# A compact recurrent state summed in TensorE, routing pieces put behind the expert units, the first gathers spread, early weight splits on GpSimd

## The chip, the cores and the metric

The kernel runs on one core of a Trainium2 chip. The metric is the device time of one execution in microseconds (us). The core has five engines that run side by side, each in the order of its own program: TensorE (PE in the rows, its weight loads PEld), VectorE (DVE), ScalarE (ACT), GpSimd (POOL) and SyncE (SP), which issues most transfers. An engine that reaches an instruction whose operands are not ready stands still, and all that is queued behind it on that engine stands too.

## The reference

Three parts follow one another (the numbers: 4 batches, 8 heads, 768 positions, head dimension 48, so 3072 tokens of 384 values):

```
state = f * state + k (x) v ;  y = q . state          # gated recurrence, per head, f = sigmoid(f_logit)
logits = x @ w_gate + softplus(x @ w_noise) * noise   # 8 experts, the two best of each token, softmax of the two
out[token] += weight * (relu(x @ w1[e]) @ w2[e])      # 384 -> 1024 -> 384 for each chosen expert
xn = x / rms(x) * g ;  (silu(xn @ wg) * (xn @ wv)) @ wo    # 384 -> 1536 -> 384 for every token
```

## The kernel before

**The recurrence** is done in 24 chunks of 128 positions, six to a batch (`gla_stream`, chunk number i). Two stages run ahead of the chunk: `decay` (VectorE `ft`, ScalarE twice, a scan on VectorE into `cs`) four chunks ahead, and `prep` (ScalarE exponentials, VectorE products `KT` and `QT`) two chunks ahead. In the chunk itself TensorE makes `scores`, transposes the next keys (`keys`), turns the last result into rows (`rows`), applies the carried state (`inter`), sums the chunk's own state (`state`) and applies the masked scores (`attend`); VectorE masks the scores (`AM`), and the state is carried on in `carry`: VectorE adds the new sum in PSUM and the old state for each half of the partitions (`su`, two instructions), GpSimd multiplies by the decay `hs` (two more). The state tile `Ss` is 128 partitions by 4 by 2 by 64 with zeros where the two heads of a pair don't meet, so that `inter` is four products over all 128 rows.

**The experts** work in units: a block is up to 512 tokens of one expert, a unit is 128 hidden columns of it. A unit has a first product `l1` (nine matmuls at 256 tokens, since a 32-bit product is done as three products of split halves, `hi` and `lo`), then ScalarE makes `hhi` and VectorE `hlo`, and two units later the second product `l2` (L646 in both). A first product needs a free PSUM bank, which the `hlo` of an earlier unit releases. Weights come in as `raw`, ScalarE makes `whi` and `wlo` is the difference (L211). Tokens of an expert are gathered from the recurrence's result `xd` by indirect transfers that GpSimd issues (L721), four to 128 tokens, then VectorE transposes them (`xt`, L732) and they are split into `xhi` and `xlo`.

**The routing** (`router`, a generator that stops at pieces) finds the two experts of each token, their places, and the lists for the gathers. It runs twice: for the first 8 chunks during the recurrence (`ahead`, one piece at each `safe()`, of which there are three to a chunk; the list ROUTE says at which chunk), and for the other 16 after it (`rest`, one piece to a unit by the list `jobs`). Both go through `route`, which raises their priority by 50. The pieces with `r_ol` and `r_rh` build one-hot tables on VectorE.

**What sets the order.** TensorE's order is the program's own (`manual_schedule`); the other engines' order is made by a list scheduler from dependences and priorities; `issue_after` keeps an instruction from being placed before another, `paced` makes a transfer wait for `mark[0]`, the last unit's `hhi`. Until the first block's tokens are there, the recurrence runs alone (`banks[0]` is BANK); then units are put between its steps in proportion to the costs that `gla_stream` yields (SHARED), and after chunk 23 the units run alone (FULL). The first block's gathers are issued from chunk FETCH on (12), its transposes at chunk 14.

## Time and profile before

| | |
|---|---|
| median of 3 runs | 1113.02 us (1111.37 to 1114.33) |
| the profiled execution | 1108.8 us, its span 1107.0 us |
| TensorE busy | 1045.5 us, 94% of the span |
| VectorE busy | 685.8 us, 62% |
| ScalarE, GpSimd busy | 483.3 us, 354.0 us |
| chain of waits that ended last | TensorE 74%, VectorE 6%, DMA 4%, issue 2% |

The shares are means over stages with different limits. In the page's 40 slices (27.7 us each) TensorE is below nine tenths in the first four, in the eighth and ninth (194 to 249 us) and in the last; elsewhere it is busy. So the stages have to be read one by one. Three of them matter here: the recurrence alone (to about 111 us), recurrence and units together (to about 207 us), and the first units alone (to about 260 us).

### The profile page before, as it was taken

To read this page: it belongs to the slowest core of one execution; us is meant where nothing else is said; L and a number is where in the kernel's file an instruction comes from. 1 tells how busy PE (TensorE), PEld (TensorE's weight loads), DVE (VectorE), ACT (ScalarE), POOL (GpSimd) and SP (SyncE) were. 2 spreads that over 40 slices of the span, in tenths; PEclk is the share of its full clock that TensorE was granted. 3 is DMA by queue.
4 is the path that set the end of the run, shared out by engine and by line. 5 is a ranking of instruction groups with operands and counts; after the bars stand their busy time and mean duration, and the time that the engine had idled before them with its cause. 6 is when DMAs were issued, how large, how long until landed. Compare 5 with 4: busy or idle time off the path is not lost.

```text
span 1107.0 us, 18624 instructions
## 1 busy us (share of the span) xinstructions
PE 1045.5 (94%) x6897; PEld 953.0 (86%) x6897; DVE 685.8 (62%) x1529; ACT 483.3 (44%) x1092; POOL 354.0 (32%) x384
## 2 busy tenths in 40 slices
PE   7885999869999999999999999999999999999997
PEld 5765899869999999999999988788888888888886
DVE  7997876688777555555676769645345444354332
ACT  6764654435665443444454544523223223232211
POOL 3344654344353434555546433220030020110000
PEclk8998899989999999999999999999999999999999
DMA  9987463357685543444353534020020110110000
GB/s 282 302 271 211 146 194 120 118 172 236 217 268 191 159 128 104 137 164 129 125 159 117 159 126 130 30 72 15 1 86 1 44 44 1 57 29 1 29 1 32
DMA packets 105256, 132.96 MB, mean 120 GB/s; under 512 B 9088, under 2 KB 81172, under 8 KB 105156
## 3 DMA queue, kind: packets, MB, share of 16 engines
q1 hardware_dynamic: 95587, 112.25, 31.5%
q0 software_dynamic: 9568, 19.43, 6.5%
q8 instruction: 56, 0.92, 0.3%
q14 instruction: 45, 0.36, 0.1%
HBM read 107.63 MB, written 24.02 MB: 119 GB/s over the span
## 4 chain that ended last, share of the span: by engine, by line
PE 74%; DVE 6%; DMA 4%; issue 2%; ACT 1%; POOL 0%; SPq 0%; DVEq 0%; ACTq 0%; POOLq 0%
PE bank L646 70%; DMA raw<-in_moe_w_dram 2%; DVE wlo L211 1%; PE bank L173 1%; DMA xg<-xd,stokr 1%; PE bank L443 1%; PE scores L379 1%; PE bank L431 1%; PE bank L421 1%; DMA xg<-xd,stoka 1%; DVE hlo L750 1%; DVE xt L732 0%; POOL xg L721 0%; DVE xlo L634 0%; DVE cv L180 0%
## 5 line engine op out<-in xcount | busy, mean ns | idle before, releaser
L646 PE MATMUL bank<-xhi,whi 128*128 128x256 f32 (+8 forms) x1008 | 339.9, 337 | 23.2 <-DVE hlo L750 13.1
L646 PE MATMUL bank<-xlo,whi 128*128 128x256 f32 (+8 forms) x1008 | 336.3, 334 | 1.3 <-DVE xlo L634 1.3
L646 PE MATMUL bank<-xhi,wlo 128*128 128x256 f32 (+8 forms) x1008 | 336.1, 333 | 0.0
L646 PE MATMUL bank<-whi,hhi 128*128 128x384 f32 (+2 forms) x728 | 247.9, 341 | 3.6 <-ACT y L766 2.3
L646 PE MATMUL bank<-whi,hlo 128*128 128x384 f32 (+2 forms) x728 | 245.6, 337 | 0.0
L646 PE MATMUL bank<-wlo,hhi 128*128 128x384 f32 (+2 forms) x728 | 245.0, 337 | 0.0
L646 PEld LDWEIGHTS bank<-xhi,whi 128*128 128x128 f32 x1008 | 191.5, 190 | 46.8 <-DVE hlo L750 15.2
L646 PEld LDWEIGHTS bank<-xlo,whi 128*128 128x128 f32 x1008 | 191.6, 190 | 17.9 <-DVE xlo L634 2.3
L646 PEld LDWEIGHTS bank<-xhi,wlo 128*128 128x128 f32 x1008 | 191.6, 190 | 17.4
L721 POOL DMA_INDIRECT xg<-xd,stokr x139 | 136.4, 981 | 151.6 <-ACT hhi L749 119.2
L750 DVE SCALAR_TENSOR_TENSOR hlo<-bank,hhi 128x256 fp32r<-128x256 f32 (+7 forms) x192 | 83.4, 434 | 112.5 <-ACT hhi L749 88.7
L211 DVE TENSOR_TENSOR wlo<-raw,whi 128x256 fp32r<-128x256 f32 (+1 forms) x296 | 135.0, 492 | 11.8 <-ACT whi L209 6.7
L209 ACT ACTIVATE whi<-raw 128x256 fp32r<-128x256 f32 (+1 forms) x320 | 128.3, 451 | 31.9 <-DMA raw<-in_moe_w_dram 23.4
L646 PEld LDWEIGHTS bank<-whi,hhi 128*128 128x128 f32 (+2 forms) x728 | 133.4, 183 | 9.7 <-ACT y L766 2.9
L646 PEld LDWEIGHTS bank<-wlo,hhi 128*128 128x128 f32 (+2 forms) x728 | 133.3, 183 | 6.2
L646 PEld LDWEIGHTS bank<-whi,hlo 128*128 128x128 f32 (+2 forms) x728 | 132.8, 182 | 3.4
L749 ACT ACTIVATE hhi<-bank 128x256 fp32r<-128x256 f32 (+7 forms) x192 | 74.7, 389 | 138.4 <-PE bank L646 116.1
L840 DVE TENSOR_TENSOR sg<-bank,sg 128x512 f32<-128x512 f32 x72 | 49.7, 690 | 118.0 <-ACT sg L839 117.9
L791 POOL DMA_INDIRECT xg<-yd,slots x40 | 44.4, 1110 | 242.7 <-ACT hhi L843 207.6
L839 ACT ACTIVATE sg<-bank 128x512 f32<-128x512 f32 x72 | 43.2, 600 | 145.4 <-PE bank L646 136.7
L843 ACT ACTIVATE hhi<-sg 128x512 fp32r<-128x512 f32 x72 | 45.4, 631 | 116.1 <-DVE sg L841 115.9
L721 POOL DMA_INDIRECT xg<-xd,stoka x64 | 70.1, 1096 | 70.0 <-ACT hhi L749 54.5
(159 smaller groups left out, 1089.4 us busy)
## 6 DMA issues: line engine op xcount, KB each, us to landing
raw<-in_moe_w_dram SPq DMA_DIRECT2D x64, 768.0 KB
kq<-in_kq_dram SPq DMA_DIRECT2D x23, 512.0 KB
yd<-y SPq DMA_DIRECT2D x48, 192.0 KB
ft<-in_f_logit_dram SPq DMA_DIRECT2D x23, 256.0 KB
Vs<-in_v_dram SPq DMA_DIRECT2D x24, 192.0 KB
xd<-x SPq DMA_DIRECT2D x24, 192.0 KB
raw<-in_moe_w_gate_dram SPq DMA_DIRECT2D x6, 768.0 KB
raw<-in_moe_w_val_dram SPq DMA_DIRECT2D x6, 768.0 KB
```

The costliest lines, as they stand in the source:

```text
L173: nc.tensor.transpose(p, x, i)
L209: nc.scalar.activation(hi[:, j], raw[:, j], AF.Copy)
L211: e.tensor_tensor(lo[:, j], raw[:, j], hi[:, j].bitcast(F32), op=OP.subtract)
L379: nc.tensor.matmul(p[:, h % 2, h // 2, :], KT[o:o + D, h // 2, :], QT[o:o + D, h // 2, :], start=True, stop=True)
L646: nc.tensor.matmul(o, a, b, start=start and i == 0, stop=stop and i == 2)
L721: paced(nc.gpsimd.indirect_dma_start(out=b.xg[i][:, k_], out_offset=None, in_=table, in_offset=bass.IndirectOffsetOnAxis(ap=rows_of[:, k_, ...
L749: mark[0] = nc.scalar.activation(hhi[:, :N], p[:, :N], AF.Relu).ins
L750: mark[1] = nc.vector.scalar_tensor_tensor(hlo[:, :N], p[:, :N], 0.0, hhi[:, :N].bitcast(F32), op0=OP.max, op1=OP.subtract).ins
L791: paced(nc.gpsimd.indirect_dma_start(out=y, out_offset=None, in_=ya if n < GROUP else yd, in_offset=bass.IndirectOffsetOnAxis(ap=at_, axis ...
L839: nc.scalar.activation(sg, ps[0], AF.Sigmoid)
L840: nc.vector.tensor_tensor(sg, ps[0], sg, op=OP.mult)
L843: mark[0] = nc.scalar.activation(hhi, sg, AF.Copy).ins
```

## The change

It has four parts.

1. **State.** `Ss` becomes 128 by 4 by 64 with one head of a pair in each half of the partitions. `state` begins with one matmul of the old state by the identity (chunks 1 to 4 of a batch), the chunk's own products are summed onto it in PSUM, and `carry` is one VectorE instruction over 128 partitions that multiplies by the last column of `cs`. `inter` becomes eight products of 48 rows and 64 columns instead of four of 128 and 128.
2. **Early work to GpSimd.** While the recurrence runs alone, all weight splits `wlo` stand on GpSimd (before, only the first third or half of each part), and so does `QT` of every odd chunk from 3 on.
3. **First gathers and routing pieces.** The last routing piece of the first run stands at chunk 11 instead of 12; the eight gathers stand in pairs, six in chunk 12 and two in chunk 13, each waiting for a `tick` (the last `AM`, `yT` or `x`); the first transpose stands at the end of chunk 13, the second at the start of 14. The yields of a chunk are 1.1, 1.1, 1.2 instead of 0.7, 0.5, 0.5, 0.5, 1.2 (3.4 both).
4. **Late routing pieces.** The second run's pieces keep their units but lose the raised priority and are placed behind the unit's `hhi` and `hlo`.

```diff
-    ROUTE, FETCH = (8, 8, 9, 9, 10, 10, 10, 11, 12), 12
+    ROUTE, FETCH = (8, 8, 9, 9, 10, 10, 10, 11, 11), 12
...
-                    e = nc.vector if j or banks[0] is FULL else nc.gpsimd
+                    e = nc.vector if banks[0] is FULL or (j and banks[0] is SHARED) else nc.gpsimd
...
-        nc.vector.tensor_tensor(st["QT", n][:, s], cs, st["kq", n][:, s, 1], op=OP.mult)
+        e = nc.gpsimd if n % 2 and banks[0] is BANK and n > 1 else nc.vector
+        e.tensor_tensor(st["QT", n][:, s], cs, st["kq", n][:, s, 1], op=OP.mult)
...
-        pU = cut(bank("U"), HP, D)
+        st["pU", n] = pU = cut(bank("U"), HP, D)
+        if c:
+            nc.tensor.matmul(pU, ident, Ss[c % 2][:, :, :D], start=True, stop=False,
+                             skip_group_check=True)
         for a in range(HP):
             for g in range(2):
                 h = 2 * a + g
                 nc.tensor.matmul(pU[64 * g:64 * (g + 1), a], Ks[n % NK][:, h],
-                                 Vs[n % NV][:, h * D:(h + 1) * D], start=True, stop=True,
-                                 skip_group_check=True)
+                                 Vs[n % NV][:, h * D:(h + 1) * D], start=not c,
+                                 stop=True, skip_group_check=True)
...
-        for g in range(2):
-            o = slice(64 * g, 64 * (g + 1))
-            wb = hs[o, n, :, None].to_broadcast([64, HP, D])
-            sn = Ss[(c + 1) % 2][o, :, g, :D]
-            if c:
-                nc.vector.tensor_tensor(t[o], u[o], Ss[c % 2][o, :, g, :D], op=OP.add)
-                st["C"] = nc.gpsimd.tensor_tensor(sn, t[o], wb, op=OP.mult).ins
-            else:
-                nc.vector.tensor_tensor(sn, u[o], wb, op=OP.mult)
+        st["C"] = nc.vector.tensor_tensor(Ss[(c + 1) % 2][:, :, :D], st["pU", n],
+                                          st["cs", n][:, :, P - 1:].to_broadcast([P, HP, D]),
+                                          op=OP.mult).ins
...
-                nc.tensor.matmul(pY[:, a, :], Ss[c % 2][:, a].rearrange("p b d -> p (b d)"),
-                                 st["QT", n][:, a, :], start=a == 0, stop=False,
-                                 skip_group_check=True)
+                for g in range(2):
+                    o = 64 * g
+                    nc.tensor.matmul(pY[o:o + 64, a, :], Ss[c % 2][o:o + D, a],
+                                     st["QT", n][o:o + D, a, :], start=a == 0, stop=False,
+                                     skip_group_check=True)
...
-        if mark[0] is not None:
+        m = mark[0] or st.get("tick")
+        if m is not None:
...
-    for i, fn in enumerate(blocks[0].fetches + [blocks[0].turns]):
-        at(FETCH + i, lambda fns=fn: [fn() for fn in fns])
+    for i, fns in enumerate(blocks[0].fetches):
+        for o in (0, 2):
+            at(FETCH + (2 * i + o // 2) // 3, lambda fns=fns[o:o + 2]: [fn() for fn in fns])
+    at(FETCH + 1, idle)
+    at(FETCH + 1, blocks[0].turns[0])
+    at(FETCH + 2, blocks[0].turns[1])
...
+    def step():
+        with behind():
+            next(rest, None)
+
     for gap in (0, 0, 0, 0, 0, 1, 0, 0, 0, 0, 2, 1, 2, 2):
-        jobs += [lambda: route(rest)] + [idle] * gap
-    jobs += [lambda: route(rest), settle]
+        jobs += [step] + [idle] * gap
+    jobs += [step, settle]
```

How this moves the instructions is seen at three places. First VectorE in the recurrence alone, about two chunks at the place where the first weights are split, before (`su` is the sum of the state, `wlo` a weight split, `lg` the routing logits):

```order
L411 TENSOR_TENSOR su<-bank_587,Ss_131 64x192 x2
L358 TENSOR_TENSOR QT<-cs,kq 128x512
L331 TENSOR_SCALAR ft<-ft 128x512
L211 TENSOR_TENSOR wlo_751<-raw,whi_750 128x256 x2
L211 TENSOR_TENSOR wlo_833<-raw,whi_832 128x256
L383 TENSOR_TENSOR AM<-scores,mask 128x1024
L337 SCALAR_TENSOR_TENSOR cs<-chain,L 128x512
L447 TENSOR_REDUCE lg<-bank_643 128x16
L352 SCALAR_TENSOR_TENSOR KT<-Ek,kq 128x512
L358 TENSOR_TENSOR QT<-cs,kq 128x512
L331 TENSOR_SCALAR ft<-ft 128x512
L211 TENSOR_TENSOR wlo_833<-raw,whi_832 128x256
```

and of the change:

```order
L409 TENSOR_TENSOR Ss_132<-bank_593,cs 128x4x48
L337 SCALAR_TENSOR_TENSOR cs<-chain,L 128x512
L384 TENSOR_TENSOR AM<-scores,mask 128x1024
L352 SCALAR_TENSOR_TENSOR KT<-Ek,kq 128x512
L446 TENSOR_REDUCE lg<-bank_646 128x16
L331 TENSOR_SCALAR ft<-ft 128x512
L359 TENSOR_TENSOR QT<-cs,kq 128x512
```

The two `su` become one product into `Ss`, the four `wlo` have gone, and of two chunks' `QT` one is left.

Second, GpSimd from the last early splits to the first block's gathers (`hs` is a copy of the decay, the DMA rows are the gathers), before:

```order
L412 TENSOR_TENSOR Ss_132<-su,hs 64x4x48
L211 TENSOR_TENSOR wlo_1324<-raw,whi_1323 128x384
L211 TENSOR_TENSOR wlo_1409<-raw,whi_1408 128x384
L412 TENSOR_TENSOR Ss_131<-su,hs 64x4x48 x2
L360 COPY hs<-cs 128x4
L412 TENSOR_TENSOR Ss_132<-su,hs 64x4x48 x2
L360 COPY hs<-cs 128x4 x2
L721 DMA xg<-xd,stoka 128x96 x8
L360 COPY hs<-cs 128x4
```

and of the change:

```order
L211 TENSOR_TENSOR wlo_1340<-raw,whi_1339 128x384
L361 COPY hs<-cs 128x4
L211 TENSOR_TENSOR wlo_1340<-raw,whi_1339 128x384
L361 COPY hs<-cs 128x4
L211 TENSOR_TENSOR wlo_1429<-raw,whi_1428 128x384 x2
L359 TENSOR_TENSOR QT<-cs,kq 128x512
L361 COPY hs<-cs 128x4 x2
L359 TENSOR_TENSOR QT<-cs,kq 128x512
L721 DMA xg<-xd,stoka 128x96 x6
L361 COPY hs<-cs 128x4
L721 DMA xg<-xd,stoka 128x96 x2
```

The products into `Ss` have gone, whole splits and `QT` have come, and the eight gathers in a row are now six and two.

Third, VectorE in the units alone, where the one-hot tables are made (`hlo` belongs to a unit; the `hlo` before this stretch stands six rows up, with table rows alone between), before:

```order
L542 TENSOR_TENSOR r_ol<-irowh,r_hf 128x1024
L546 TENSOR_TENSOR r_rh<-r_rh,names 128x448
L544 TENSOR_TENSOR r_rh<-irowh,r_hf 128x448
L542 TENSOR_TENSOR r_ol<-irowh,r_hf 128x1024
L546 TENSOR_TENSOR r_rh<-r_rh,names 128x448
L544 TENSOR_TENSOR r_rh<-irowh,r_hf 128x448
L732 STREAM_TRANSPOSE xt<-xg 128x384
L546 TENSOR_TENSOR r_rh<-r_rh,names 128x448
L211 TENSOR_TENSOR wlo_3052<-raw,whi_3051 128x256
L634 TENSOR_TENSOR xlo_3043<-xt,xhi_3042 128x3x128
L211 TENSOR_TENSOR wlo_3052<-raw,whi_3051 128x256 x2
L750 SCALAR_TENSOR_TENSOR hlo<-bank_3061,hhi 128x256
```

and of the change, beginning with a unit's `hlo`:

```order
L750 SCALAR_TENSOR_TENSOR hlo<-bank_3116,hhi 128x256
L541 TENSOR_TENSOR r_ol<-irowh,r_hf 128x1024
L543 TENSOR_TENSOR r_rh<-irowh,r_hf 128x448
L541 TENSOR_TENSOR r_ol<-irowh,r_hf 128x1024
L545 TENSOR_TENSOR r_rh<-r_rh,names 128x448
L543 TENSOR_TENSOR r_rh<-irowh,r_hf 128x448
L211 TENSOR_TENSOR wlo_3143<-raw,whi_3142 128x384
L545 TENSOR_TENSOR r_rh<-r_rh,names 128x448
L211 TENSOR_TENSOR wlo_3143<-raw,whi_3142 128x384
L750 SCALAR_TENSOR_TENSOR hlo<-bank_3150,hhi 128x256
```

Before, all four pairs of tables stand between two `hlo`; now two stand behind the first `hlo`, and the other two behind one `hlo` each.

## Rows read from the trace of the kernel before

**Rows 1.** Busy time by stage: header names columns; start:end, length, engines, clock, DMA.
```profile
core 0: us, PE busy (x) PEld busy (x) DVE busy (x) ACT busy (x) POOL busy (x), PEclk, DMA share, GB/s
...
24.20:67.10 42.90, 35.41 (x450) 30.62 (x448) 42.02 (x65) 32.93 (x68) 15.19 (x24) 1.00 0.99 299
...
67.10:102.90 35.80, 27.38 (x343) 24.08 (x342) 33.75 (x97) 20.38 (x41) 15.35 (x16) 0.90 0.79 231
...
102.90:111.20 8.30, 1.19 (x19) 1.00 (x17) 4.49 (x9) 2.79 (x5) 6.14 (x8) 0.80 0.67 214
...
111.20:125.00 13.80, 12.88 (x101) 11.72 (x101) 11.15 (x20) 7.67 (x18) 7.22 (x8) 0.75 0.44 129
...
125.00:207.00 82.00, 80.75 (x817) 74.97 (x818) 57.31 (x100) 44.05 (x103) 43.41 (x53) 1.00 0.50 161
```

**Rows 2.** TensorE's waits: us in total, times, longest.
```profile
PE bank L646 <- DVE hlo L750: 13.1, 5, 8.8
...
PE bank L646 <- ACT xhi L633: 9.3, 3, 7.1
```

**Rows 3.** VectorE by line, 8 to 111 us: count, busy us, mean ns, idle before.
```profile
L358 DVE TENSOR_TENSOR QT<-cs,kq 128x512 f32<-128x512 f32 x15 | 11.2, 745 | 0.1
...
L331 DVE TENSOR_SCALAR ft<-ft 128x512 f32<-128x512 f32 x17 | 8.3, 494 | 0.0
...
L411 DVE TENSOR_TENSOR su<-bank,Ss 64x192 f32<-64x192 f32 x18 | 6.3, 351 | 0.4 <-PE bank L394 0.2
...
L211 DVE TENSOR_TENSOR wlo<-raw,whi 128x256 fp32r<-128x256 f32 x8 | 3.5, 481 | 0.0
...
L211 DVE TENSOR_TENSOR wlo<-raw,whi 128x384 fp32r<-128x384 f32 x4 | 2.2, 546 | 0.0
...
L414 DVE TENSOR_TENSOR Ss<-bank,hs 64x192 f32<-64x192 f32 x6 | 2.1, 352 | 1.3 <-PE bank L394 1.2
```

**Rows 4.** The same view of VectorE, 24.2 to 67.1 us.
```profile
L352 DVE SCALAR_TENSOR_TENSOR KT<-Ek,kq 128x512 f32<-128x512 f32 x7 | 6.4, 911 | 0.0
```

**Rows 5.** The same view of VectorE, 67.1 to 102.9 us.
```profile
L352 DVE SCALAR_TENSOR_TENSOR KT<-Ek,kq 128x512 f32<-128x512 f32 x5 | 3.4, 685 | 0.0
```

**Rows 6.** GpSimd by line, 24.2 to 67.1 us.
```profile
L412 POOL TENSOR_TENSOR Ss<-su,hs 64x192 f32<-64x192 f32 x10 | 7.2, 718 | 9.3 <-DVE su L411 8.9
...
L211 POOL TENSOR_TENSOR wlo<-raw,whi 128x256 fp32r<-128x256 f32 x4 | 3.7, 920 | 4.5 <-ACT whi L209 4.5
...
L211 POOL TENSOR_TENSOR wlo<-raw,whi 128x384 fp32r<-128x384 f32 x2 | 2.5, 1280 | 1.8 <-ACT whi L209 1.8
```

**Rows 7.** TensorE in order of time: start, length, line, operation, idle before.
```profile
26.67 1.07 PE L421 MATMUL bank<-QT,Ss 128*128 128x128 f32 x8
```

**Rows 8.** TensorE's weight loads in order of time.
```profile
24.20 0.97 PEld L379 LDWEIGHTS scores<-QT,KT 48*128 48x128 f32 x16 [0.17 <-issue]
```

**Rows 9.** GpSimd in order of time, the first block's gathers.
```profile
101.81 0.95 POOL L721 DMA_INDIRECT xg<-xd,stoka  x1 [0.30 <-issue]
...
106.81 0.94 POOL L721 DMA_INDIRECT xg<-xd,stoka  x1 [0.30 <-issue]
```

**Rows 10.** VectorE in order of time, the first block's transpose.
```profile
106.62 0.69 DVE L732 STREAM_TRANSPOSE xt<-xg 128x384 f32<-128x384 f32 x1 [4.80 <-DMA xg<-xd,stoka]
```

**Rows 11.** VectorE in order of time, the routing pieces of the second half.
```profile
231.35 1.22 DVE L542 TENSOR_TENSOR r_ol<-irowh,r_hf 128x1024 f16<-128x1024 f16 x1
...
232.48 0.62 DVE L544 TENSOR_TENSOR r_rh<-irowh,r_hf 128x448 f16<-128x448 f16 x1
...
242.21 0.42 DVE L750 SCALAR_TENSOR_TENSOR hlo<-bank,hhi 128x256 fp32r<-128x256 f32 x1
```

**Rows 12.** TensorE in order of time, the same place.
```profile
242.69 0.58 PE L646 MATMUL bank<-xhi,whi 128*128 128x256 f32 x1 [8.82 <-DVE hlo L750]
...
248.18 0.28 PE L646 MATMUL bank<-xhi,wlo 128*128 128x256 f32 x1
...
250.29 0.28 PE L646 MATMUL bank<-xhi,wlo 128*128 128x256 f32 x1
```

40 lines of the change are left out of this document (17 added, 23 removed).

## The prediction

> **What bounds the kernel now.** I read the page's slices first (where TensorE is not full), then the busy time by stage, TensorE's waits, and for the stages found the groups by line and the instructions in order of time. From 125 to 207 us TensorE is busy 80.75 of 82.00 us [rows 1], and the page's slices say the same from 249 us on: there its own work is the time, and what the change does on other engines is worth nothing. The time to be had lies in two places.
>
> The first is the recurrence alone. From 24.2 to 67.1 us VectorE is busy 42.02 of 42.90 us and TensorE 35.41; from 67.1 to 102.9 it is 33.75 of 35.80 against 27.38 [rows 1]. VectorE is the bound, so work taken off it shortens the stage until another limit shows: TensorE's busy time, or the transfers, which are at 0.99 and 299 GB/s up to 67 us. Then come 8.3 us in which no engine is full [rows 1]: TensorE waits 7.1 us for the first block's `xhi` [rows 2], since VectorE waits 4.80 us for gathers before it can transpose [rows 10]. The clock is then 0.75 in the next stretch [rows 1].
>
> The second is the stage after the recurrence: 13.1 us of waits for `hlo`, 8.8 of them at once [rows 2]. In front of that `hlo` VectorE works 10.9 us, from 231.35 to 242.21, nearly all of it routing tables [rows 11]. TensorE stands 8.82 us and starts again at half rate, 0.58 us for a matmul that takes 0.28 at 248.18 [rows 12].
>
> **The change part by part.** *A, the recurrence alone.* I compare what stands on VectorE ahead of the second transpose. Gone are 18 `su` (6.3 us), 6 products into `Ss` (2.1), 8 and 4 `wlo` (3.5 and 2.2) and 6 of 15 `QT` (6 times 0.745, 4.5): 18.6 us [rows 3]. New are 12 `carry` over all partitions. No row shows one; it has as many columns as a `su`, so 0.35 us each from there, between 0.35 and 0.70, the two it replaces: I take 4.2 us, since halves of the partitions run at the same length in both lines [rows 3]. The order also brings one `KT` (0.7) [rows 5] and four `ft` (2.0) [rows 3] ahead of this point. Net 11.7. VectorE's instructions overlap by 0.09 us (1.22 long, the next 1.13 later) [rows 11], and 25 fewer give 2.2 of it back: 9.5.
>
> Against this, GpSimd slows VectorE: a `KT` takes 0.911 us on average up to 67 us and 0.685 after [rows 4, 5], and `ft` and `QT` are longer too. I put the whole at about 3.8 us for 15.19 us of GpSimd [rows 1], a quarter. GpSimd loses 18 products (about 0.7 each, 13 us) and gains 12 splits (about 1.0 each) and 6 `QT`; a split of 256 columns takes 0.92 and of 384 1.28 [rows 6], so 512 columns come to about 1.6, between 1.28 and 2 times 0.92. That is 22 us more and 13 less; a quarter of 9 is 2.2. A is -9.5 + 2.2, and -7.5 is taken. TensorE allows it: 62.8 us busy in the 78.7 from 24.2 to 102.9 [rows 1], some 4 more for the identity. The transfers allow less: 12.8 MB (299 GB/s by 42.9 us) must land in the first stretch; so 0 is the upper end of A, and -12 the lower (no GpSimd cost, `carry` at 0.35).
>
> The Trainium skill's page "SBUF — State Buffer", section "SBUF: two separate sides", says that VectorE (with two SBUF inputs, or in a two-port mode) and GpSimd take a shared port pair as a lock for a whole instruction, and the other stops fully. The rows bear out that they hinder one another, at a quarter of GpSimd's time and not all of it; by the full lock A would be a loss, which is the last rival.
>
> *B, the first block.* The fourth gather's issue ends at 102.76 us [rows 9] and the transpose starts at 106.62 [rows 10]: 3.9 us to land. Now six gathers are issued in chunk 12; the last two wait for chunk 13's `AM`, take 1.25 each (106.81 less 101.81 over four) [rows 9] and 3.9 to land: 6.4 us after that `AM`. The next chunk's scores end about 4.3 us after it (6.1 us a chunk now, seven in 42.9 [rows 1], less about 0.6 from A and 1.2 for the `AM`). So the second transpose is 2.1 us late, and transpose and `xhi` add 1.2 (0.69 [rows 10] and a little less on ScalarE): TensorE waits some 3 us instead of 7.1, B = -4, between 0 and -7. Behind a gather that waits for its tick, GpSimd holds only `hs` copies and splits for later units; a scan needs such a copy two chunks later, which covers it. The last routing piece a chunk earlier costs nothing by itself: it is the same work on a busy VectorE.
>
> *C, the clock.* The 13.8 us after the wait have 0.75 [rows 1]; a quarter at the cost of half gives 3.4 us of lost work. A shorter wait may save it or not: -1.5, between 0 and -3.4.
>
> *D, recurrence and units together.* Here TensorE is full, so its new work counts whole. The identity is two instructions of 192 columns; `inter` shows 1.07 us for eight of 128 [rows 7], 1.04 ns a column, so 0.40 us, seven times after chunk 14: 2.8. `inter` itself has twice the matmuls of half the width and half the rows: between half its time and twice, I take the same. Between matmuls of different tile shapes a gap of 0.17 us stands [rows 8]; `inter` now differs from its neighbours, so up to two more gaps in eight chunks, 2.7; I take 0.7. D = +3.5, between 0 and +6. VectorE has time there (57.31 of 82.00) [rows 1], which hides the longer `QT` of before and the scan.
>
> The Trainium skill, page "TensorEngine Tiling (Array Packing)", section "Key Properties", states that a change of tile mode drains the engine. The gap before `scores` agrees with it; by that rule both gaps are due in every such chunk, and D would be 5.5.
>
> *E, the routing pieces.* A unit takes 2.11 us of TensorE (250.29 less 248.18) [rows 12]. By the new order two table pairs stand behind one `hlo`: 2 times 1.13, 4 times 0.54 (0.62 less overlap), two splits of 0.47 and the `hlo` of 0.34, 5.7 us [rows 3, 11]. The next two have one pair and three splits of 0.40: 3.75 each. Together 13.2 against three units' 6.3: 6.9 us late. Two gaps just ahead carry both transposes, some 3.2 each, 2.2 more; about one unit is slack. So some 7 us of waits remain of the 13.1, in pieces; about 1 more comes later, where the pieces for the ranking now lie close to two transposes. -5. The half rate after the long wait cost half of 5.5 us (242.69 to 248.18), 2.7; whether waits of 1 to 4 us bring it too is open. E = -5 without it; the ends are +2 (as late, and at half rate throughout) and -13. VectorE's total is the same: what is behind a unit now is late for the next one, not gone.
>
> Smaller memsets, priorities of the first transposes and the yields (3.4 both times) cost nothing that a row shows: GpSimd's memsets lie ahead of its first product, and the transposes' place is priced in B.
>
> Sum: -7.5 - 4 - 1.5 + 3.5 - 5 = -14.5 us on the profiled execution's 1108.8, or 1094.3. That execution is 4.2 us under the median of 1113.0 us; on the median the sum gives 1098.5, and I say 1098.
>
> **Rivals.** *The transfers bind* (A = -1). For it: 0.99 up to 67 us. Against it: no wait of VectorE for `ft` stands there (0.0) [rows 3], and the share is 0.79 after [rows 1], so a lead can be used up and won back. B would be -3 and C nothing: -1 - 3 + 3.5 - 5 = -5.5, 1107.5 us.
>
> *The routing waits only move* (E = 0). For it: VectorE does the same 10.9 us of tables, at 2.3 us a piece above a unit's 2.11. Against it: other units lie between. -9.5, 1103.5 us.
>
> *Pieces behind units are hidden fully* (E = -13). For it: the units' `wlo` have a lead. Against it: the 5.7 us gap. -22.5, 1090.5 us.
>
> *Slower: GpSimd locks VectorE out.* Place: chunks 3 to 14. Price: all 22 us of new GpSimd work stop VectorE, the old 13 us give back a quarter (3.2): A = -9.5 + 22 - 3.2 = +9.3; the first block's gathers stand in the same queue, so B and C are 0; with D and E the sum is +7.8, 1121 us. It decides from about two thirds: at 0.65 of the 22 us the sum is nothing. For it: `KT` at 0.911. Against it: the quarter read above.
>
> **How the numbers follow.** Chances: forecast 0.46, transfers 0.15, waits that move 0.20, hidden fully 0.11, slower 0.08. The forecast's own bounds (A -10 to -4, B -6 to -2, D 2 to 6, E -8 to -2) give 1089 to 1107; 1088 to 1112 leaves the slower case and the far end of the hidden one out. What this kernel's runs can tell from no change is about 0.3%, 3.3 us: faster is under 1109.7. The forecast, the moved waits, the hidden case and somewhat over half of the transfers' case are faster, 0.84, of which I keep 0.82; same 0.10; slower 0.08.
>
> **What would show it.** A: scores of chunk 14 at about 95 us instead of 102.9, VectorE still above nine tenths, `KT` near 0.9 us. B: a wait for `xhi` of about 3 us. D: a line of identity matmuls at 0.2 us each and TensorE full. E: waits for `hlo` of about 7 us, none above 4. The prediction is wrong if VectorE waits for `kq` or `ft` before 67 us, if GpSimd's lines double in length, or if TensorE's first unit comes later than 105 us.

## The result: 0.7% slower, where 1.4% faster was forecast

The changed kernel's median is 1119.17 us (1118.40 to 1123.39, six runs) against 1113.20 us (1111.15 to 1114.33) of the kernel before beside it: ratio 1.0067, 95% interval 1.0046 to 1.0088. A second measurement on another chip gave 1.0081 (1.0052 to 1.0111). The profiled execution of the change took 1118.4 us, its span 1116.6, 9.6 more than before. The forecast was 1098 us, with 1088 to 1112 as its range: the sign is wrong.

The same five stretches after, which answer to [rows 1] (columns: stretch, its length, busy time and instructions of TensorE, its weight loads, VectorE, ScalarE and GpSimd, granted clock, DMA share, GB/s):

```profile
24.20:67.10 42.90, 39.47 (x542) 32.91 (x540) 35.35 (x50) 32.85 (x69) 23.81 (x28) 1.00 0.98 297
67.10:102.90 35.80, 27.60 (x326) 23.68 (x323) 29.57 (x84) 17.33 (x36) 10.67 (x13) 0.81 0.77 227
102.90:111.20 8.30, 5.77 (x71) 4.99 (x69) 3.39 (x7) 4.38 (x9) 6.61 (x8) 0.92 0.72 213
111.20:125.00 13.80, 10.66 (x87) 8.66 (x86) 7.70 (x16) 6.05 (x13) 4.86 (x7) 0.68 0.34 101
125.00:207.00 82.00, 78.47 (x841) 70.69 (x841) 52.89 (x90) 43.57 (x102) 31.68 (x38) 1.00 0.44 139
```

VectorE is relieved, as meant: 35.35 us busy up to 67.1 us where it was 42.02, 29.57 where it was 33.75. TensorE is the busier one now, 39.47 for 35.41. But from 67 to 103 us its clock is 0.81 where it was 0.90, and from 111 to 125 us 0.68 where it was 0.75.

TensorE's costliest waits [rows 2], the identity and the waits for `yT`, by line (busy time and mean ns, then idle time ahead and its releasers):

```profile
L645 PE MATMUL bank<-xhi,whi 128*128 128x256 f32 (+8 forms) x1008 | 339.6, 337 | 14.5 <-DVE hlo L750 10.3 <-ACT xhi L632 3.9
...
L442 PE MATMUL bank<-columns,yT 128*128 128x112 f32 x192 | 27.6, 290 | 6.2 <-ACT yT L435 6.1
...
L395 PE MATMUL bank<-Ss,ident 128*128 128x192 f32 x32 | 9.9, 392 | 0.0
```

The waits for `xhi` fell from 9.3 to 3.9 us and those for `hlo` from 13.1 in five to 10.3 in ten, and still the end is later. A fixed event in each stage tells where. Read from the two traces in order of time:

| from, to | before | after | difference |
|---|---|---|---|
| start, `scores` of chunk 2 | 24.2 | 26.6 | +2.4 |
| chunk 2, chunk 9 | 42.9 | 40.9 | -2.0 |
| chunk 9, chunk 12 | 25.8 | 30.2 | +4.4 |
| chunk 12, first unit's matmul | 18.3 | 17.9 | -0.4 |
| first unit, 25th `hlo` | 109.7 | 112.8 | +3.1 |
| 25th `hlo`, 49th `hlo` | 65.3 | 65.1 | -0.2 |
| 49th `hlo`, TensorE's end | 813.4 | 815.0 | +1.6 |

The sum is 8.9, and 0.7 more stands behind TensorE's end. The second profile of the change has 28.4, 39.6, 28.6, 18.8, 112.8, 65.4 and 819.0 us in these rows: two executions of the same kernel differ by up to 1.8 us in one of the first six rows and by 4.0 in the last, so the last row says nothing. The third (+4.4, and +2.9 in the second profile) is the largest loss of the first six in the first profile, in a stretch to which the prediction gave a gain. Every ratio below is against the kernel before in runs on the same chip, as the chips differ (its median was 1107 to 1113 us on them).

What stands on TensorE in that stretch, in order of time (start, length, what, [idle before]), before:

```profile
83.50 1.07 PE L421 MATMUL bank<-QT,Ss 128*128 128x128 f32 x8
88.19 0.53 PE L552 MATMUL bank<-r_rh,r_ol 128*128 128x56 f16 x8 [3.63 <-DVE r_rh L546]
90.52 0.53 PE L552 MATMUL bank<-r_rh,r_ol 128*128 128x56 f16 x8 [1.79 <-DVE r_rh L546]
90.98 1.97 PE L431 MATMUL bank<-AM,Vs 128*64 128x128 f32 x16
92.88 1.81 PE L379 MATMUL scores<-QT,KT 48*128 48x128 f32 x16
```

and in the change:

```profile
83.87 1.16 PE L380 MATMUL scores<-QT,KT 48*128 48x128 f32 x16
89.58 0.55 PE L551 MATMUL bank<-r_rh,r_ol 128*128 128x56 f16 x8 [4.55 <-DVE r_rh L545]
91.78 0.53 PE L551 MATMUL bank<-r_rh,r_ol 128*128 128x56 f16 x8 [1.64 <-DVE r_rh L545]
92.13 1.09 PE L173 MATMUL bank<-ident,KT 128*128 128x128 f32 x4
93.02 1.89 PE L442 MATMUL bank<-columns,yT 128*128 128x112 f32 x8
94.83 1.72 PE L420 MATMUL bank<-QT,Ss 48*64 48x128 f32 x16
...
96.68 1.09 PE L430 MATMUL bank<-AM,Vs 128*64 128x128 f32 x16
97.70 1.16 PE L380 MATMUL scores<-QT,KT 48*128 48x128 f32 x16
```

TensorE waits 4.55 and 1.64 us for `r_rh`, and only then come `keys` (ident,KT), `rows` (columns,yT) and `inter` (QT,Ss) of the chunk, at half rate. Before, these three stood ahead of the wait, and only `attend` behind it. The loss stands there: the second `r_rh` product starts 23.4 us behind the scores of chunk 9 before, and 24.3 and 23.4 us in the two profiles of the change, so the tables came no earlier on the relieved VectorE; from it to the scores of chunk 12 it takes 2.4 us before, 5.9 and 5.3 in the change. In the same stretch, 69 to 79 us show a shorter wait and the half clock behind it:

```profile
69.00:71.00 2.00, 0.20 (x2) 0.00 (x0) 1.61 (x5) 2.00 (x5) 0.90 (x1) 1.00 1.02 300
71.00:73.00 2.00, 1.79 (x16) 1.69 (x18) 1.97 (x22) 2.00 (x6) 0.50 (x2) 0.82 0.89 259
73.00:75.00 2.00, 2.00 (x14) 1.35 (x10) 2.00 (x8) 1.29 (x3) 1.45 (x3) 0.50 0.94 269
...
77.00:79.00 2.00, 2.00 (x20) 1.67 (x18) 1.57 (x6) 0.99 (x2) 0.63 (x1) 0.50 0.25 79
79.00:81.00 2.00, 2.00 (x30) 1.77 (x29) 1.07 (x1) 0.87 (x2) 0.00 (x0) 0.98 0.87 243
```

TensorE stands 2.0 us until 71.2 (it waits for `yT`; on ScalarE a `whi` that waits 2.85 us for its `raw` stands in front), and then it runs at 1.2 GHz, half rate, from 72 until 79. The second profile has no half clock there, and its second `r_rh` product is 0.9 us nearer to the scores of chunk 9. By that the half clock cost no more than 0.9 us here: TensorE waits for the tables anyway.

At the first gathers, VectorE's side and GpSimd's (which answers to [rows 9, 10]):

```profile
97.21 0.28 DVE L611 TENSOR_SCALAR stoka<-bank,quad 128x64 int32<-128x64 f32 x1
98.91 1.23 DVE L384 TENSOR_TENSOR AM<-scores,mask 128x1024 f32<-128x1024 f32 x1 [1.42 <-PE scores L380]
...
109.43 0.69 DVE L732 STREAM_TRANSPOSE xt<-xg 128x384 f32<-128x384 f32 x1 [4.91 <-DMA xg<-xd,stoka]
```
```profile
100.45 1.41 POOL L721 DMA_INDIRECT xg<-xd,stoka  x1 [0.17 <-issue]
...
110.17 1.35 POOL L721 DMA_INDIRECT xg<-xd,stoka  x1 [0.30 <-issue]
```

The list `stoka` is written at 97.5, but the first gather starts at 100.45, right behind the `AM` of chunk 12 that ends at 100.14: the tick that the change made the gathers wait for. Before it took 0.3 us from `stoka`'s end at 96.76 to the first gather at 97.05.

After the recurrence, the single wait of 8.82 us [rows 12] is gone. Of the ten waits for `hlo`, which are spread from 132 to 610 us, these three stand in its place:

```profile
242.00 0.39 PE L645 MATMUL bank<-xhi,whi 128*128 128x256 f32 x1 [0.55 <-DVE hlo L750]
...
245.17 0.39 PE L645 MATMUL bank<-xhi,whi 128*128 128x256 f32 x1 [0.80 <-DVE hlo L750]
...
250.85 0.58 PE L645 MATMUL bank<-xhi,whi 128*128 128x256 f32 x1 [3.29 <-DVE hlo L750]
```

The 31st `hlo` comes only 0.2 us later than before, 7.3 us won since the 25th; by the 49th all of it is lost again, since the tables that stood ahead of one `hlo` now stand behind several, and some waits for `y` and a half clock (0.77 from 252 to 262 us) come in.

### The profile page after: what moved, and what is told of

Same layout as the page of the kernel before. It is cut to its first block, busy times and chain, and to the rows that moved or that the text cites. A ratio compares the mean times of both kernels' runs of the same rounds, so it can differ in the third digit from the quotient of the medians.

```text
span 1116.6 us, 18933 instructions
## 1 busy us (share of the span) xinstructions
PE 1060.1 (95%) x7089; PEld 959.3 (86%) x7089; DVE 666.1 (60%) x1488; ACT 482.1 (43%) x1092; POOL 350.5 (31%) x373
## 5 line engine op out<-in xcount | busy, mean ns | idle before, releaser
L645 PE MATMUL bank<-xhi,whi 128*128 128x256 f32 (+8 forms) x1008 | 339.6, 337 | 14.5 <-DVE hlo L750 10.3
L645 PEld LDWEIGHTS bank<-xlo,whi 128*128 128x128 f32 x1008 | 191.2, 190 | 18.4 <-DVE xlo L633 2.7
L645 PEld LDWEIGHTS bank<-xhi,wlo 128*128 128x128 f32 x1008 | 191.4, 190 | 17.3
L211 DVE TENSOR_TENSOR wlo<-raw,whi 128x256 fp32r<-128x256 f32 (+1 forms) x282 | 126.6, 484 | 18.1 <-ACT whi L209 10.1
L843 ACT ACTIVATE hhi<-sg 128x512 fp32r<-128x512 f32 x72 | 45.4, 631 | 115.8 <-DVE sg L841 115.6
```

The source lines that it names most:

```text
L211: e.tensor_tensor(lo[:, j], raw[:, j], hi[:, j].bitcast(F32), op=OP.subtract)
L645: nc.tensor.matmul(o, a, b, start=start and i == 0, stop=stop and i == 2)
L843: mark[0] = nc.scalar.activation(hhi, sg, AF.Copy).ins
```

## The experiments

The theory after the comparison was that each of the four parts had a hidden cost: TensorE as the new bound, GpSimd's queue, the routing piece's place, waits that move. The first four runs undo one part each.

**The state as before**

```diff
-        st["C"] = nc.vector.tensor_tensor(Ss[(c + 1) % 2][:, :, :D], st["pU", n],
...
+                nc.vector.tensor_tensor(t[o], u[o], Ss[c % 2][o, :, g, :D], op=OP.add)
+                st["C"] = nc.gpsimd.tensor_tensor(sn, t[o], wb, op=OP.mult).ins
```

> The changed kernel with the state as it was before (su on VectorE, two products on GpSimd, state with both groups side by side, no identity matmul, inter with 128 rows); the other parts stay. Theory 1 (the compact state makes TensorE the bound of a chunk, so that every wait of some 2 us costs half clock, and it adds 3 us of identity matmuls behind chunk 14): about 1112 us, 7 below the changed kernel's 1119, scores of chunk 9 at about 67 us again and no half clock at 72 to 79. Rival (the compact state is the part that helps, VectorE being full without it): 1125 us or more, scores of chunk 9 at 69 us or later.

Ratio 1.0073 (1.0048 to 1.0098), no better than the change: the expected 1112 us, 0.999 of the kernel before, was missed, and the scores of chunk 9 came at 74.6 us, the rival's sign. Chunk 2 to 9 took 50.4 us: TensorE waited 6.7 us for `Ss` from GpSimd, which was busy 33.4 us in that stretch (24.2 in the change, 15.2 before). So the splits and `QT` on GpSimd live only on the room that the compact state makes there. Behind the first unit this run was 4.7 to 8.3 us faster than two with the identity (104.5 us to the 25th `hlo` against 109.2 in the last of these four and 112.8 in the change), which bears out the sign of D but not its size, since more of the recurrence lay ahead of its late first unit.

**`QT` and the early `wlo` back on VectorE**

```diff
-                    e = nc.vector if banks[0] is FULL or (j and banks[0] is SHARED) else nc.gpsimd
+                    e = nc.vector if j or banks[0] is FULL else nc.gpsimd
...
-        e = nc.gpsimd if n % 2 and banks[0] is BANK and n > 1 else nc.vector
-        e.tensor_tensor(st["QT", n][:, s], cs, st["kq", n][:, s, 1], op=OP.mult)
+        nc.vector.tensor_tensor(st["QT", n][:, s], cs, st["kq", n][:, s, 1], op=OP.mult)
```

> The changed kernel with QT of the odd chunks and the early wlo back on VectorE. Theory 1 (GpSimd takes its instructions in order, so a QT there that waits for its scan holds up the scans of VectorE at 67.8 us and the first gathers at 100.45 us): first gather at about 97.5 us, first unit about 3 us earlier, about 1114 us. Rival (taking this work off VectorE is what gains, and the loss is elsewhere): chunks of 6.1 us again, first unit 4 us later, 1123 us.

1.0050 (1.0023 to 1.0077). The first gather came at 97.96, again right behind an `AM` (96.45 to 97.68) and 2.9 us behind the end of `stoka`: so it is the tick that holds the gathers, not `QT`. Chunk 2 to 9 took 42.6 us, 1.7 more than the change's first profile, chunk 9 to 12 27.9, 2.3 less. What VectorE gives away is worth next to nothing as a whole.

**Gathers and early routing pieces as before**

```diff
-    ROUTE, FETCH = (8, 8, 9, 9, 10, 10, 10, 11, 11), 12
+    ROUTE, FETCH = (8, 8, 9, 9, 10, 10, 10, 11, 12), 12
...
-        m = mark[0] or st.get("tick")
...
```

> The changed kernel with the early routing pieces, the first block's gathers, their waits and the priority of the first transposes as before. Theory 1 (the last early routing piece, a chunk earlier, now stands on TensorE ahead of keys, rows and inter of chunk 12, so the same 6 us wait of TensorE for r_rh has less work in front of it): first r_rh wait again with keys, rows and inter ahead of it, scores of chunk 12 about 2 us earlier than 97.7, but the last two gathers later, together about 1118 us. Rival (the spread gathers gain their 4 us as predicted, and the loss is elsewhere): TensorE waits 7 us for the first xhi again, 1123 us.

1.0030 (1.0010 to 1.0051), the best of the four. Chunk 9 to 12 took 26.8 us instead of 30.2 and 28.6, and from the second `r_rh` product to the scores of chunk 12 it is 2.4 us again: this part holds most of the loss.

**Late pieces as before**

```diff
...
-        jobs += [step] + [idle] * gap
+        jobs += [lambda: route(rest)] + [idle] * gap
...
```

> The changed kernel with the late routing pieces as before (each with priority, not behind the unit). Theory 1 (the pieces' waits only move: 4.4 us won at the eighth hlo after 230 us are lost again by 266 us): 1119 us, within 2 us of the changed kernel. Rival (the pieces behind units gain 5 us as predicted): 1124 us, with one wait of some 9 us for hlo.

1.0046 (1.0026 to 1.0065); not told apart from the change on the whole. The stretch that the part is about says it: 25th to 49th `hlo` 65.2 us, 65.1 with the part and 65.3 before. E is nothing.

The next four ask what bounds a chunk, and what the half clock costs.

**The identity twice, and the sum on VectorE**

```diff
+            for _ in range(2):
+                nc.tensor.matmul(pU, ident, Ss[c % 2][:, :, :D], start=True, stop=False,
...
```
```diff
-            nc.tensor.matmul(pU, ident, Ss[c % 2][:, :, :D], start=True, stop=False,
...
+            nc.vector.tensor_tensor(t, u, Ss[c % 2][:, :, :D], op=OP.add)
```

> The changed kernel with the identity matmul issued twice in every chunk (the second overwrites the first). Theory 2 (with the compact state TensorE bounds a chunk of the recurrence alone, so VectorE's relief is not paid out): from the scores of chunk 2 to those of chunk 9 (40.9 us in the changed kernel) 7 times 0.5 more, some 44 us, and 3 to 4 us more again behind chunk 14: about 7 us above the changed kernel, ratio to the kernel before 1.013. Rival (VectorE or the transfers still bound a chunk): 41 us from chunk 2 to 9, only the part behind chunk 14 is longer, ratio 1.010.

> The changed kernel with the compact state summed on VectorE (an add and a product over all partitions, 0.35 us each) in place of the identity matmul. Theory 2: TensorE loses 0.5 us a chunk and VectorE, at 0.83 in 25 to 75 us, has room for 0.35: chunk 2 to 9 in about 38 us, 3 us less behind chunk 14, ratio to the kernel before about 1.001. Rival (VectorE is still as good as full, since its instructions wait on one another): chunk 2 to 9 in 41 us or more, ratio 1.006.

Twice: 1.0116 (1.0089 to 1.0143), between the two numbers expected. On VectorE: 1.0053 (1.0033 to 1.0074), the rival's number. From chunk 2 to 9 in the change, with the identity twice, and with the sum on VectorE (columns as above):

```profile
26.59:67.45 40.86, 37.43 (x508) 31.38 (x507) 34.27 (x48) 31.30 (x66) 24.16 (x28) 1.00 0.97 296
```
```profile
24.94:73.02 48.08, 44.55 (x519) 38.22 (x517) 34.01 (x49) 34.73 (x74) 24.68 (x30) 0.86 0.97 283
```
```profile
25.74:66.21 40.47, 34.69 (x498) 30.00 (x496) 36.05 (x52) 31.87 (x67) 24.87 (x28) 1.00 0.95 290
```

In the change TensorE is busy 37.43 of 40.86 us, 0.92. In five of these seven chunks the identity stands. Chunks 2 and 3 of the change alone (from a chunk's scores to the next one's):

```profile
26.59:32.19 5.60, 5.60 (x81) 4.80 (x79) 5.42 (x7) 3.65 (x7) 1.65 (x3) 1.00 1.09 322
32.19:38.82 6.63, 5.86 (x81) 4.82 (x79) 6.16 (x11) 6.05 (x12) 0.45 (x2) 1.00 0.89 274
```

In chunks 2 and 7 TensorE does not stand at all, in 4 and 5 for 0.3 to 0.4 us, in 3, 6 and 8 for 0.8 to 1.2 us, mostly ahead of `rows`, where it waits for `yT`. Before, it was VectorE that stood for at most 0.36 us in any of these chunks. So VectorE's relief was paid out until TensorE's own work (5.6 us in a chunk with the identity) or its wait for `yT` stood next.

With the identity twice TensorE does not stand at all in five of the seven chunks. But the 7.2 us that it takes longer are not the added work itself: they lie in chunks 3, 6 and 7 (26.1 us, 17.3 in the change), at clocks of 0.68, 0.71 and 0.87 behind waits of 1.49 and 2.04 us for `yT`; the other four take 1.5 us less than in the change. Without the identity TensorE is busy 34.69 us, 2.7 less, and 0.4 us is won: it then stands 1.2 to 1.9 us in each of four chunks, for `yT` and `AM`, which come from ScalarE and VectorE. So TensorE is not the only bound either.

**Matmuls on ones in the waits, in the change and in the kernel before**

```diff
+            if n0 == 0 and j in (0, 8):
+                fill(6 if j else 20)
             nc.tensor.matmul(pt_, ol[:, j], rh[:, j], start=j == 0, stop=j == 2 * ng - 1)
...
+            if pid == f == t0 == 0:
+                fill(8, p)
```

> The changed kernel with idle-time matmuls on ones in TensorE's waits: 20 ahead of the first r_rh product, 6 ahead of the second (a wait of 4.55 and one of 1.64 us), 8 ahead of the first unit. If the half clock after these waits costs time: TensorE at full clock from 90 to 97 us, scores of chunk 12 some 3 us earlier, ratio 1.003. Rival (the routing pieces, not TensorE, set the time here): scores of chunk 12 earlier, but the table stoka and the first unit where they were, ratio 1.007.

> The kernel before with such matmuls on ones: 16 ahead of the first r_rh product, 6 ahead of the second, 28 ahead of the first unit (waits of 3.6, 1.8 and 7.1 us). If the half clock after the waits costs time: full clock from 90 to 95 us and from 111 to 118 us, 2 to 3 us and 3.4 us, ratio 0.995. Rival (gates, tables and gathers set the time up to the first unit; only the units behind it gain): 0.997. If the clock falls in spite of them, or they delay the products: 1.000 or above.

In the change 1.0041 (1.0021 to 1.0061): chunk 9 to 12 took 27.4 us at clock 1.00, where the change has 30.2 at 0.77 in the first profile and 28.6 at 0.88 in the second. So 1 to 3 us of the loss there are the half clock: from the second `r_rh` product to the scores of chunk 12 it takes 4.0 us at full clock, 5.3 to 5.9 in the change. In the kernel before 1.0068 (1.0042 to 1.0093), slower: chunk 9 to 12 came down from 25.8 to 24.7, but the 28 matmuls ahead of the first unit took 7.98 us and began late, since TensorE had work until then:

```profile
109.21 1.68 PE L379 MATMUL scores<-QT,KT 48*128 48x128 f32 x13 [0.83 <-issue]
110.82 7.98 PE L1010 MATMUL bank<-ones 128*128 128x512 bf16 x28
118.45 0.47 PE L648 MATMUL bank<-xhi,whi 128*128 128x256 f32 x1
```

The row ahead of them shows something new: products of chunks 13 and 14 have waits of up to 0.83 us that no engine explains ("issue", 2.7 us in all), while GpSimd issues the eight gathers (97.57 to 107.81 here) and until 1.4 us behind the last. In the change the same was there, 2.9 us from 107 to 113.

**Without the tick, more loads, the tick and ones, the change again**

```diff
-        m = mark[0] or st.get("tick")
+        m = mark[0]
```
```diff
+        if 5 <= n <= 11:
+            x = ld.tile([P, HP, P], F32, name="sp", bufs=1)
+            nc.sync.dma_start(x, f_logit[b, :, :, c * P:(c + 1) * P].rearrange(
...
```

> The changed kernel with the first block's gathers no longer waiting for the last tick of the recurrence (a mask product, yT or x); their place in the program stays. Theory 3 (this wait, which the change adds, holds the first gather from the table stoka, ready at 97.5 us, until the mask product of chunk 12 ends at 100.1 us, and the first unit hangs on the gathers): first gather some 0.6 us behind stoka, first unit about 3 us earlier, ratio to the kernel before 1.004 where the changed kernel has 1.0067. Rival (the gathers would land behind the chunk's loads anyway): the first transpose still 12 us behind stoka, ratio 1.007.

> The changed kernel with a load of 256 KB more, into a tile that nothing reads, beside the gates of chunks 5 to 11. If the transfers bind the recurrence alone (one of the rivals on record): 1.84 MB more at some 313 GB/s, 5.9 us, and scores of chunk 9 some 5 us later than without. If TensorE or VectorE bind: scores of chunk 9 within 1.5 us, ratio 1.007 to 1.009.

> The changed kernel without that wait of the gathers and with matmuls on ones ahead of the two r_rh products (20 and 6), none ahead of the first unit. Theory 3 and the clock together: first unit 3 us earlier by the wait and up to 3 by full clock from 90 to 97 us; ratio 1.001 to 1.002. Rival (the two hide one another, since the gathers and not TensorE lead to the first unit): 1.004, as without the wait alone.

> The changed kernel as it is, for a second profile and a ratio on the chip of the three runs beside it. Expected 1.0067 again. If the waits of TensorE that no engine explains (2.9 us from 107 to 113 us) belong to the program, they are there again; if they belong to one execution or one chip, not.

The change again: 1.0081. Without the tick: 1.0066 (1.0041 to 1.0092), nothing gained, though the gathers came as the theory said: first gather 0.3 us behind `stoka`'s end, first transpose 8.4 us behind `stoka` (12.2 in the change). TensorE lost it meanwhile:

```profile
102.63 0.36 DVE L409 TENSOR_TENSOR Ss<-bank,cs 128x192 f32<-128x192 f32 x1 [2.71 <-remote]
...
104.55 0.68 DVE L732 STREAM_TRANSPOSE xt<-xg 128x384 f32<-128x384 f32 x1
...
108.59 1.23 DVE L384 TENSOR_TENSOR AM<-scores,mask 128x1024 f32<-128x1024 f32 x1 [3.06 <-remote]
```
```profile
99.22 0.67 PE L400 MATMUL bank<-Vs,Ks 128*64 128x48 f32 x16
...
100.71 0.89 PE L380 MATMUL scores<-QT,KT 48*128 48x128 f32 x8
...
106.98 2.05 PE L442 MATMUL bank<-columns,yT 128*128 128x112 f32 x8 [2.49 <-issue]
...
114.56 1.66 PE L380 MATMUL scores<-QT,KT 48*128 48x128 f32 x16
```

VectorE's `Ss` waits 2.71 us and its `AM` 3.06 for products that TensorE had begun at 99.22 and at 100.71, and from the scores of chunk 13 to those of 14 it takes 13.9 us (5.2 before); chunk 13 goes on only at 106.98, when the gathers (96.74 to 107.60) are about out. Theory 3 falls here: with gathers that start earlier, the recurrence stands earlier. With ones ahead of `r_rh` as well: 1.0028 (1.0011 to 1.0046); chunk 9 to 12 took 27.6 us, which is the clock's part again.

More loads: 1.0173 (1.0149 to 1.0198). Chunk 2 to 9 took 45.1 us, 4.3 more, and chunk 9 to 12 another 4.8. Here VectorE waits for a transfer, `kq`, 1.90, 3.03 and 0.81 us, and 4.1 of the 4.3 us lie in chunk 5, which ran at clock 0.69 behind a wait of 1.84 us for `yT`. In the two traces of the change neither VectorE nor TensorE waits over 0.4 us for a transfer from chunk 2 to 12; ScalarE does, for weights (`raw`): 0.7 and 0.9 us up to chunk 9, 2.85 and 2.1 behind it. So more transfers would bind; as far as these waits tell, those of the change reach the recurrence through ScalarE's weight copies alone.

**Fewer loads, plain loads, the early plan alone**

```diff
+            if nm == "v" and n >= NV:
+                continue
```
```diff
+            if t0 == e == 0:
+                nc.sync.dma_start(b.xg[i][:, k_], table[(4 * i + k_) * P:(4 * i + k_ + 1) * P])
+                return
```

> The changed kernel without the value loads from chunk 5 on (older values are used again), 0.2 MB less a chunk of some 1.8. If the transfers bind the recurrence alone: from the scores of chunk 2 to those of chunk 9 some 4 us less, 36.5 to 37.5 us. If TensorE binds (39.5 of 42.9 us busy): 40 us or more.

> The same in the kernel before. If VectorE binds there (42.0 of 42.9 us busy), as the prediction had it: chunk 2 to 9 in 42 us or more. If the transfers bind there too: 38 to 39 us.

> The changed kernel with the first block's eight gathers replaced by eight plain loads of fixed rows on SP's queue (the first block computes on other rows; all the rest is as it was). If the gathers cause TensorE's unexplained waits: none of more than 0.2 us from 95 to 115 us, and, since the first unit then waits for neither the routing table nor the gathers, first unit a little behind the scores of chunk 14, at about 108 us, 7 us before the changed kernel's: ratio to the kernel before 1.000. Rival (the waits belong to the point of the program, for instance the place in the instruction stream): the same 3 to 5 us in the products of chunks 13 and 14, ratio 1.004.

> The kernel before with the last early routing piece a chunk earlier and the gathers' place and priority of the change, without the gathers' wait for a tick, and with nothing else of the change. Theory 3: the table stoka comes 2 to 4 us earlier against the scores of chunk 12, which come 2 us later; first unit 1 to 2 us earlier, ratio 0.998 to 1.000. Rival (the piece ahead of keys, rows and inter costs TensorE what the table gains): 1.002.

The two kernels with fewer value loads compute on older values, so they serve as measurements only. With fewer value loads the change took 43.1 us from chunk 2 to 9, not 37: the DMA share stayed at 1.01, so other loads took the place, and chunk 4 took 8.9 us instead of 5.6, behind a wait of 2.1 us for `yT` and at clock 0.81; from chunk 5 to 9 it was 22.0 us where the change has 23.0 and 22.3. The kernel before did it in 42.3, as VectorE's bound has it. So the transfers cost when there are more of them, but are not the one bound either. Ratios 1.0051 (1.0027 to 1.0075) and 0.9997 (0.9976 to 1.0017).

With plain loads of fixed rows the ratio is 0.9975 (0.9955 to 0.9996), the one kernel faster than before, but its first block leaves out the routing's choice of rows. From chunk 12 to the first unit it took 13.4 us, 18.7 in the run with gathers and fewer value loads on the same chip, and the scores of chunks 12, 13 and 14 follow one another by 6.7 and 5.6 us. The three runs with gathers on that chip showed no "issue" waits of TensorE at this place either, so this run can't tell what makes them; that the first unit is some 5 us earlier when neither the table nor the gathers stand in front of it, it does show.

The early plan alone in the kernel before: 0.9992 (0.9971 to 1.0013). Chunk 12 to the first unit came down from 18.3 to 14.1 us, and chunk 9 to 12 went up from 25.8 to 29.3: what the table gains, the order on TensorE loses. So on this chip, where the unexplained waits don't show, an earlier table and gathers without the tick do win some 4 us (18.1 us in the run of the kernel before with fewer value loads beside it).

**The plan mended: `r_rh` behind `inter`, the table still a chunk earlier, no tick**

```diff
-        m = mark[0] or st.get("tick")
+        m = mark[0]
...
-    for i in (8, 9):
+    for i in (8, 9, 11):
         at(i, idle)
```

> The kernel before with the last early routing piece in chunk 11, but the product of r_rh behind keys, rows and inter as before; gathers placed as in the change, without a wait for a tick. If the order on TensorE is what the early plan costs: chunk 9 to 12 in about 26 us, scores of chunk 12 to the first unit in 14 to 15 us (18.3 before), ratio 0.996. Rival (the half clock comes after the wait for r_rh wherever the product stands): 28 us or more, ratio 0.999 to 1.001.

> The changed kernel with the same mended plan and no wait for a tick: what is left is the compact state, the work moved to GpSimd, the yields and the late pieces. If the order on TensorE and the gathers' wait were the loss: 1.000 to 1.002, between the 1.007 of the changed kernel and 0.996. If the compact state and GpSimd's work lose by themselves: 1.004 or more.

In the kernel before 1.0000 (0.9984 to 1.0015), in the change 1.0048 (1.0028 to 1.0067). Chunk 9 to 12 took 26.0 and 26.4 us. So the order on TensorE is what the early piece costs, 3.3 us in the kernel before (29.3 less 26.0, on two chips), 2.2 to 3.8 in the change (28.6 and 30.2 less 26.4); from the second `r_rh` product to the scores of chunk 12 it is 2.6 and 2.3 us with the mended plan, 5.9 with the early piece in the kernel before. But chunk 12 to the first unit took 18.4 and 23.0 us: as without the tick, the recurrence stands while the early gathers (93.73 to 103.71 in the second) are issued. Of that run, TensorE and ScalarE:

```profile
86.33 1.09 PE L420 MATMUL bank<-QT,Ss 48*64 48x128 f32 x16
87.64 0.37 PE L551 MATMUL bank<-r_rh,r_ol 128*128 128x56 f16 x8 [0.22 <-DVE r_rh L545]
...
97.68 1.06 PE L430 MATMUL bank<-AM,Vs 128*64 128x128 f32 x16
...
105.82 2.05 PE L442 MATMUL bank<-columns,yT 128*128 128x112 f32 x8 [5.40 <-ACT yT L435]
```
```profile
105.17 0.60 ACT L435 ACTIVATE yT<-bank 128x512 f32<-128x512 f32 x1 [7.74 <-remote]
```

`inter` stands ahead of `r_rh`, and the wait for it is 0.22 us. But `attend` of chunk 12, at 97.68, gives its result to ScalarE only at 105.17, 1.5 us behind the last gather, and TensorE waits 5.40 us for that `yT`. No other kernel was measurably faster than the kernel before.

## Why the prediction was wrong

**A, the recurrence alone: this step failed,** forecast -7.5, measured +4.8 at chunk 12 (+2.4 - 2.0 + 4.4), in three ways.

*Up to chunk 9* the gain is real but 2.0 us (3.3 in the second profile): seven of eight other runs with the same work took 39.6 to 41.3 us from chunk 2 to 9, the eighth 42.3, against 42.6 to 42.9 in four traces with the kernel before's work. "TensorE allows it" was the mistake. VectorE's busy time in the first stretch fell by 6.67 us, and I set most of such a saving down as time: 62.8 + 4 us of TensorE's work against the 71 that were to be left, 0.94 on average. In single chunks there was no such room: the sum makes a chunk 5.5 us, and TensorE's own work is 5.6 in one with the identity. The gain ended with TensorE at 0.92, full in some chunks and waiting for `yT` in others. Taking the identity away moved the bound and won 0.4 us; what makes `yT` late is shown only for two of the waits, where ScalarE stood for `raw` in front of it.

*At chunk 1* 2.4 us were lost at half clock: TensorE waited 1.84 us for `KT`, until 20.5, and ran at half rate from 21 to 25 us. In other runs with the compact state chunk 1 took 0.6 to 4.5 us longer than the 7.0 of the kernel before, in four others of the kernel before's work none to 2.8: much of it comes with the execution, and I had no term for it.

*From chunk 9 to 12* the sentence that failed is that the last routing piece a chunk earlier "costs nothing by itself: it is the same work on a busy VectorE". It is, on VectorE; on TensorE it stood ahead of three pieces of the chunk, which then ran behind its wait instead of in front of it. It cost 2.2 to 3.8 us, half clock included, by the runs with the plan and with it mended. And VectorE's relief won nothing here: the second `r_rh` product came 23.4 to 24.3 us behind the scores of chunk 9, before and after, and 21.9 with `QT` and the splits back on VectorE.

That GpSimd locks VectorE out for all its new work, the slower rival, did not happen, though its time was nearly right: added up from chunk 2 to 9, what VectorE's instructions take above the shortest of their own line is 4.5 us before, and 4.8 and 2.6 in the two profiles of the change, with 24 us of GpSimd beside them instead of 15. A quarter of GpSimd's time was the wrong measure, as [rows 1], [rows 4] and [rows 5] could have told: `KT` is at 0.685 us where GpSimd is busy 15.35 of 35.80 us. What counts is which instruction meets which, before (two rows) and in the change (the next two, and `KT` by line):

```profile
42.56 1.23 DVE L352 SCALAR_TENSOR_TENSOR KT<-Ek,kq 128x512 f32<-128x512 f32 x1
42.52 0.73 POOL L211 TENSOR_TENSOR wlo<-raw,whi 128x256 fp32r<-128x256 f32 x1 [1.07 <-ACT whi L209]
```
```profile
42.10 0.68 DVE L352 SCALAR_TENSOR_TENSOR KT<-Ek,kq 128x512 f32<-128x512 f32 x1
42.12 1.26 POOL L211 TENSOR_TENSOR wlo<-raw,whi 128x256 fp32r<-128x256 f32 x1 [3.59 <-ACT whi L209]
```
```profile
L352 DVE SCALAR_TENSOR_TENSOR KT<-Ek,kq 128x512 f32<-128x512 f32 x8 | 6.1, 764 | 0.0
```

The one that starts second is the longer by about what is left of the first: a `KT` of 0.68 us takes 1.15 to 1.28 behind a running split in three of seven cases before, 1.32 in one of eight in the change; where `KT` is first, the split pays, 1.26 us instead of 0.73. The Trainium skill, page "SBUF — State Buffer", section "SBUF: two separate sides", states just this, that whichever of the two starts first has the shared port pair for its whole instruction while the other is blocked. The trace agrees with it; the rival went wrong in taking every new microsecond of GpSimd for such a meeting.

**B, the first block: failed.** Forecast -4, measured -0.4 from chunk 12 on. I counted when the gathers may be issued and not the added wait of the first for its chunk's `AM`, 2.7 us. Where that wait is taken away, the earlier start wins 4 us in the one run on a chip on which TensorE runs on beside the gathers; on the two on which chunks 13 and 14 lose it again, chunk 12 to the first unit took 17.3 to 23.0 us in four runs, 18.3 before. I had set the gathers beside the recurrence as if they cost it nothing. The wait for `xhi` did become 1.86 us, by TensorE's being late.

**C, the clock: failed with A and B.** TensorE ran at half rate from 108 to 118 us before and from 110 to 120 in the change, as long. The 13.8 us behind the first unit's start have 0.84 and 0.77 in the two profiles instead of 0.75 only because part of the half rate now lies ahead of it: the waits in the products of chunks 13 and 14 stand ahead of the fall, where the wait for `xhi` stood before.

**D, recurrence and units together: as forecast in the change, its size not settled.** +3.5 forecast, +3.1 in both profiles; but ten other runs with one identity had -1.1 to +3.5, and the one with the sum on VectorE, without it, +1.6, so the agreement may be luck. The changed yields, which place the units between the recurrence's steps here, were undone in no run. The two identity matmuls take 0.52 us (from 105.33 to the next product at 105.85) and not 0.40; `inter` in its sixteen instructions takes 1.09 us at full clock against 1.07 [rows 7]. More gaps ahead of weight loads are there (5.1 us of "issue" in 26 from 116 to 220 us, 1.5 in 6 before), but whether they cost TensorE time isn't shown.

**E, the late pieces: failed,** -5 forecast, -0.2 measured, and 0 with the part undone. The tables were sized about right (the three `hlo` behind them came 5.68, 3.54 and 3.55 us apart, 5.7, 3.75 and 3.75 by the sum). The step that failed is that nearly half of the waits would be gone: between the 25th and the 49th `hlo` TensorE stood 9.5 us before and 7.7 after, 6.0 for `hlo` and 1.7 for `y`, for which the sum had no term, and the stretch is as long. The rival that the waits only move was right: VectorE's tables are the same work, and the units behind them had too little lead to hide it.

Of the signs, the one to watch was on record: TensorE's first unit later than 105 us (115.6). VectorE above nine tenths did not come either: 35.35 of 42.90 us, 0.82.

## What to carry to other kernels

When the fullest engine is relieved, compare the time that is to be left with the next engine's work in a single step, not on average over the stretch: here TensorE was at 0.92 on average and already full in single chunks. An engine that waits and works in turn has a falling clock to lose besides. A step moved earlier must be followed on every in-order engine that it issues to, here TensorE, whose products of the moved piece were taken for nothing. And a transfer that starts earlier is only won when what runs meanwhile doesn't wait for it or on it: measure what the overlap costs.
